# Zero matmuls ahead of TensorE's waits, forced ScalarE table switches, and a fully biased first batch in a fused attention and token-mixing kernel

## The chip, the cores and the metric

The kernel runs on one core of a Trainium2 chip. The metric is the device time of one execution, in microseconds (us). The kernel before took 180.71 us, the median of 8 runs that lie between 179.4 and 184.47 us. One execution was profiled. In the profile, PE is TensorE's matmul path, PEld its weight loads, DVE is VectorE, ACT ScalarE, POOL GpSimd and SP the queue engine. [...]

## The reference

Four batches of eight heads, 768 rows and a head width of 64 go through a sparse attention: a row sees the 8 global columns and the last 96 rows up to itself, with a bias that falls linearly with the distance. The attention's output, as a 768 by 512 matrix per batch, goes through a mixing block.

```
scores = scale * q @ k.T - slope[h] * dist        # masked to 8 global + 96 local columns
a = exp(scores) / sum(exp(scores));  x = a @ v     # per head, then heads side by side
theta = x @ w_theta                                # 512 x 512
y = w_tok_r @ (x * cos(theta)) + w_tok_i @ (x * sin(theta))   # 768 x 768 each
u = x + y
out = u + relu(u @ w_ch)                           # 512 x 512
```

## The kernel before, in words

**Tiling.** A batch `b` is cut into six tiles of 128 rows, and these into three groups `g` of two tiles. Heads are taken in four pairs `p`. Names of operations carry these numbers: `s012` is the score operation of batch 0, group 1, pair 2.

**A batch's operations.** `t` transposes q or k on PE (L377), and `q`, `k`, `kp` copy the result out of PSUM (L386); `kg` writes the global columns into it (L399). `s` computes scores (L452), `x` is the exponential on ACT (L475), `v` multiplies with the values on PE (L504), and `n` normalises on DVE (L515, L517). `vpa` and `vpb` build the previous tile's values (L413, L416). `xt` and `xc` transpose the result (L529, L532; by DMA in the last two batches). `th` is the matmul with w_theta (L547), `cos` and `sin` run on ACT (L556, L558), `z` multiplies on DVE (L568). `tw` and `twc` transpose the token weights once (L337, L342). `mx` is the token mixing (L589), `u` the sum (L601), `ut` and `uc` its transpose (L612, L616, or a DMA at L620), `ch` the channel matmul (L631), `o` the final step on DVE (L637) and `st` the store.

**The bias.** It comes into the scores in one of two ways. In a biased group (`BIASED`, groups 0 and 1 of batch 0) two matmuls `bi` per head pair put a multiple of a distance table `dtab` into PSUM first (L444), and the scores accumulate on it. Everywhere else, `m` multiplies the exponentials by a table `etab` = exp(-slope * dist) on DVE (L483). `etab` is made by eight activations at the start (L672).

**What sets the order.** The program is a flat list of operation names, `ORDER`, issued one by one; each name falls to one engine's queue, and a suffix such as `/ACT` chooses the engine of a copy. [...] The attributes `prio`, `lat`, `after` and `boost` belong to the planner that wrote the list and do nothing at run time. Loads go through POOL's queue in the order `load1` to `load81`; from `load20` a `gate` (L216) holds POOL until the load five places earlier has landed. Stores and DMA transposes go through SP's queue.

**Buffers.** PSUM has two rings of four banks, `pa` (scores and theta) and `pb` (all else). An operation that takes a bank waits for the reader of the bank's last user.

**The start.** `warm0` is eight matmuls of zeros (L326) while the first loads are under way. The first q and k tiles come as float32 over the SP and ACT queues (`hw`, L266) and are cast by `cast` (L273).

Of the kernel before, what the change touches and what calls it, by code (L numbers as in the profile page):

```python
# [15 lines left out]
class Plan:  # L16
# [3 lines left out]
    def __init__(self, pools):  # L20
        self.pools, self.ops = pools, {}
# [5 lines left out]
    def issue(self, order):  # L27
        assert sorted(n.split("/")[0] for n in order) == sorted(self.ops)
        for n in order:
            n, _, eng = n.partition("/")  # L30
            op = self.ops[n]
            op.took = eng or op.took
            op.fn()
# [3 lines left out]
hw00 hw10 ones1 zero rel ones2 halfpi ones3 warm0 ones4 ones6 ones0 ones5 load1 hw01 hw11 sid4 sid2 sid5 sid7  # L37
sid3 sid1 load2 sid0 sid6 far0 ident far1 load3 dtab0 cast00/DVE dtab1 load4 dtab2 cast10/DVE t0000 q000/DVE
load5 t0010 dtab3 k000/DVE kp000/ACT bi0000 bi0001 load6 bi0010 etab2 bi0011 kg000 cast01/DVE etab5 load7
t0001 cast11/DVE q001/ACT t0011 load8 etab7 kp001/DVE etab4 k001/DVE load9 kg001 etab6 s000 s001 load10 x0000  # L40
x0001 bi0020 load11 x0010 t0100 x0011 bi0021 s002 q010/DVE etab3 load12 t0110 x0020 bi0030 bi0031 k010/DVE
x0021 s003 load13 bi0100 etab1 kp010/DVE bi0101 load14 etab0 vpa00/DVE kg010 vpb00/DVE x0030 s010 load15 x0031
v002 v001 x0100 v000 load16 v003 vpa01/DVE x0101 bi0110 n000 bi0111 load17 s011 vpb01/DVE bi0120 load18 x0110
bi0121 n002 s012 x0111 load19 n003 bi0130 v010 x0120 bi0131 n001 s013 x0121 n010 t0200 x0130 t0210 x0131
q020/DVE v011 v013 k020/DVE kp020/ACT v012 n013 xt00 vpa02/DVE kg020 vpb02/DVE s020 xc00/DVE s021 x0200 n011
gate20 x0210 load20 n012 x0201 tw00 x0211 gate21 s022 m020 load21 twc00/ACT s023 m021 v020 x0220 xt01 n020
x0221 v021 gate22 th001 xc01/DVE load22 x0230 m022 x0231 th000 gate23 m023 load23 v022 cos000 tw10 n021 v023
gate24 twc10/DVE th010 load24 n023 gate25 tw11 n022 load25 th011 sin000 twc11/DVE cos001 gate26 z000 xt02
load26 sin001 tw01 xc02/DVE cos010 gate27 z001 twc01/ACT load27 th021 sin010 gate28 t1010 cos011 load28 z010
tw20 mx000 sin011 k100/DVE gate29 kp100/ACT load29 twc20/DVE tw21 th020 gate30 twc21/DVE load30 kg100  # L50
vpa10/DVE mx010 cos020 gate31 z011 load31 sin020 t1000 vpb10/DVE cos021 mx001 gate32 q100/DVE load32 sin021
z020 mx011 z021 gate33 s100 load33 s101 mx012 x1000 x1001 gate34 load34 x1010 mx002 m100 x1011 u01 gate35 s102
load35 s103 m101 x1020 u00 x1021 gate36 v100 x1030 load36 v101 n100 x1031 tw31 gate37 t1100 m102 twc31/ACT
load37 ut01 m103 t1110 q110/ACT uc01/DVE v102 gate38 k110/DVE v103 load38 ut00 kp110/DVE uc00/ACT tw40 tw30
gate39 kg110 twc40/DVE ch00 load39 twc30/ACT n102 tw41 gate40 n101 mx020 load40 twc41/DVE o00 s110 gate41
mx021 load41 vpa11/DVE x1100 st00 vpb11/DVE x1101 mx022 gate42 n103 load42 m110 xt10 u02 s111 gate43 xc10/ACT
load43 v110 t1200 n110 gate44 x1110 ut02 ch01 load44 q120/DVE x1111 uc02/DVE gate45 s112 m111 load45 s113
x1120 ch02 o01 gate46 x1130 load46 t1210 st01 x1121 o02 tw50 x1131 mx040 k120/DVE gate47 st02 kp120/ACT load47
m113 tw51 mx041 twc50/DVE gate48 twc51/ACT load48 kg120 m112 v113 s120 n113 gate49 v112 load49 x1200 mx050
n112 x1201 vpa12/DVE gate50 s121 m120 load50 s122 x1210 mx042 vpb12/DVE x1220 gate51 v120 x1221 load51 u04  # L60
mx052 x1211 m122 gate52 ut04 mx051 load52 uc04/DVE m121 v122 gate53 ch04 u05 load53 n120 v121 gate54 ut05 n122
v111 load54 uc05/ACT mx030 n121 n111 gate55 s123 load55 th101 vpa20/DVE x1230 vpb20/DVE x1231 gate56 o04 xt11
load56 th100 m123 xc11/ACT st04 gate57 v123 load57 cos100 mx032 n123 gate58 th110 load58 xt12 sin100 gate59
mx031 cos101 xc12/DVE load59 sin101 z100 ch05 gate60 cos110 u03 load60 th121 sin110 o05 gate61 th120 vpa21/DVE
load61 st05 vpb21/DVE t2010 z101 gate62 t2100 load62 k200/DVE kp200/ACT t2000 q210/DVE t2110 gate63 load63
th111 q200/DVE k210/ACT kp210/DVE t2200 gate64 cos111 load64 kg200 ut03 kg210 q220/DVE mx110 uc03/ACT gate65
z110 sin111 ch03 load65 cos120 z111 mx100 sin120 gate66 o03 load66 cos121 z120 t2210 st03 sin121 mx101 gate67
k220/DVE kp220/ACT load67 z121 s200 s201 gate68 mx111 vpa22/DVE x2000 load68 kg220 x2001 vpb22/DVE x2010 mx102
m200 gate69 x2011 load69 s202 m201 s203 mx112 u10 x2020 gate70 x2021 load70 x2030 ut10 v201 u11 v200 x2031
gate71 m202 s210 load71 ut11 n200 mx120 x2100 n201 gate72 x2101 mx121 load72 m203 m210 v203 gate73 s211 load73  # L70
vpa30/DVE v210 n203 x2110 mx122 gate74 x2111 n210 load74 s212 vpb30/DVE s213 u12 x2120 ch10 gate75 x2130 m211
load75 ut12 v202 x2121 ch11 o10 x2131 gate76 m212 load76 st10 s220 n202 v211 x2200 mx140 gate77 m213 x2201
load77 xt20 s221 n211 v212 gate78 m220 x2210 mx142 load78 x2211 n212 v220 m221 s222 gate79 load79 ch12 n220
x2220 x2221 vpa31/DVE gate80 s223 load80 vpb31/DVE v221 x2230 m222 mx130 x2231 gate81 n221 load81 v222 mx132
m223 n222 gate82 v223 load82 v213 n223 th201 n213 xt22 th200 o12 o11 mx131 cos200 xt21 mx150 u13 st12 mx152
sin200 ut13 vpa32/DVE cos201 mx151 z200 sin201 st11 mx141 u15 vpb32/ACT z201 th221 ut15 u14 th220 ut14 t3110
t3210 k310/DVE kp310/ACT th210 k320/DVE t3010 kp320/DVE cos210 t3000 k300/DVE sin210 t3100 q300/ACT kp300/DVE
th211 q310/DVE ch15 cos211 kg300 kg310 z210 sin211 ch14 o15 cos220 t3200 z211 sin220 st15 ch13 cos221 o14
sin221 z220 mx200 st14 q320/DVE s300 z221 s301 mx201 x3000 kg320 x3001 o13 x3010 mx202 m300 x3011 st13 s302
m301 s303 mx210 u20 x3020 x3021 x3030 ut20 v300 m302 mx212 x3031 n300 s310 m303 s311 x3100 mx211 x3110 v301  # L80
x3111 u21 mx220 x3101 n301 ut21 ch20 m311 s312 m310 s313 x3120 mx222 o20 x3121 st20 v303 x3130 mx221 m312
x3131 n303 v310 v311 u22 v312 ch21 n310 ut22 n312 mx240 o21 v302 mx242 n302 st21 n311 mx230 xt30 m313 s320
s321 x3200 mx231 x3210 v313 x3211 mx232 n313 x3201 m321 ch22 xt31 u23 s322 m320 s323 ut23 x3220 mx250 o22
x3230 v320 x3231 mx241 st22 n320 x3221 m323 mx252 u24 v323 m322 th300 ut24 n323 v322 cos300 v321 n322 th301
n321 mx251 xt32 sin300 ch23 u25 cos301 z300 ch24 sin301 ut25 o23 th310 z301 st23 th311 o24 cos310 sin310 st24
mx300 cos311 z310 th320 sin311 z311 th321 cos320 sin320 mx301 cos321 z320 mx310 sin321 z321 mx311 mx302 mx312
u30 ch25 ut30 u31 mx320 o25 ut31 mx322 st25 mx321 ch30 u32 mx330 ut32 o30 mx331 st30 mx332 ch31 u33 mx340 ut33
o31 ch32 st31 mx342 o32 mx341 st32 mx350 u34 mx352 ut34 mx351 ch33 u35 ut35 o33 ch34 uc35/ACT st33 ch35 o34
ch351 o35 st34 o351 st35 st351
# [4 lines left out]
def kernel(  # L94
# [44 lines left out]

    def act_t(n):  # L140
        return 0.06 + n * 0.00084
# [14 lines left out]
    BIASED = (0,1)  # L156
# [12 lines left out]
    zero = const.tile([T, 512], BF, name="zero")  # L169

    add("zero", {"DVE": 0.3}, lambda: nc.vector.memset(zero, 0.0), writes=["zero"], prio=-9)
    for i in range(NV):
        add(f"ones{i}", {"DVE": 0.07},
            lambda i=i: nc.vector.memset(v_bufs[i][:, :, :, D:D + 1], 1.0), writes=[("ones", i)], prio=-8)
    add("halfpi", {"DVE": 0.07}, lambda: nc.vector.memset(halfpi, math.pi / 2.0), writes=["halfpi"], prio=-8)
# [33 lines left out]
    def load(fn, us, ndesc, spot, depth=0, reads=(), writes=(), alloc=None):  # L209
# [4 lines left out]
        if depth:  # L214
            add(f"gate{n}", {"POOL": 0.35},
                lambda: nc.gpsimd.tensor_copy(out=scrap, in_=landed[n - depth]()),  # L216
                reads=[("ld", n - depth)], prio=-100 + n - 0.5, after=after)
            after = [f"gate{n}"]
        add(f"load{n}", {"POOL": 0.62 + 0.00028 * ndesc}, fn, reads=reads, writes=list(writes) + [("ld", n)],
            alloc=alloc, prio=-100 + n, lat=(1.05, us + {2: 0.75, 3: 0.75, 17: 1.1}.get(n, 0.0), 0.65), after=after)  # L220

    def load_qk(b, g, i, t, depth=0):
        key = ("qk", b, g)

        def fn():
            if key not in tiles:
# [501 lines left out]
```

## Time and profile before

| what | value |
|---|---|
| median of 8 runs | 180.71 us |
| the profiled execution's own time | 179.4 us |
| its span, first to last instruction | 177.6 us |
| PE busy | 161.3 us, 91% |
| DVE busy | 134.4 us, 76% |
| ACT busy | 107.0 us, 60% |
| POOL busy | 84.0 us, 47% |
| mean granted TensorE clock | 0.976 |

The profiled execution is the fastest of the eight. Its time is 1.8 us longer than its span. Matmuls overlap in the pipeline, so a busy PE is not a PE at its peak; how much work it does in a stretch is better counted in matmuls of a known pitch.

### The profile page before, as it was taken

The page shows a single profiled execution, that of the slowest core. Times are in us where ns is not written, and L with a number is a line of the kernel's source. Part 1 is how long each engine was busy: PE and PEld are TensorE (multiplying, and loading weights), DVE is VectorE, ACT ScalarE, POOL GpSimd, SP SyncE. Part 2 cuts the span into 40 slices and gives each one's busy share as a digit, 9 for nine tenths or more (in the row PEclk, how much of TensorE's full clock was granted, in tenths as well). Part 3 has the DMA queues.
Part 4 walks back from the last instruction along what each step waited for, and adds up shares of the span by engine and source line. Part 5 has one row for each costly group of instructions (what it writes and reads, how often), then busy time and mean ns, then how long its engine had stood idle before and what let it go on. Part 6 is the DMA issues. An engine that isn't in the chain of part 4 may idle for free.

```text
span 177.6 us, 4008 instructions
## 1 busy us (share of the span) xinstructions
PE 161.3 (91%) x1529; PEld 89.9 (51%) x1552; DVE 134.4 (76%) x315; ACT 107.0 (60%) x183; POOL 84.0 (47%) x150
## 2 busy tenths in 40 slices
PE   7469979898999999999697999999999999999991
PEld 2145656564856564474353554664554554444440
DVE  7726899887999988689599896798696787543442
ACT  2398869979937737858945667299741674600010
POOL 8998279849979999899799000000000000000000
PEclk9957999999999999999999999999999999999998
DMA  5999999999999999999999919404135656124514
GB/s 123 187 154 151 194 177 130 154 175 132 145 123 191 221 133 126 169 152 124 164 125 137 196 30 202 127 10 167 33 89 135 104 93 165 42 47 114 183 45 177
DMA packets 96868, 23.73 MB, mean 134 GB/s; under 512 B 91088, under 2 KB 93904, under 8 KB 96848
## 3 DMA queue, kind: packets, MB, share of 16 engines
q0 software_dynamic: 73504, 12.33, 97.0%
q1 hardware_dynamic: 21264, 10.62, 23.4%
q10 hardware_dynamic: 2080, 0.52, 1.6%
q8 instruction: 12, 0.20, 0.4%
q14 instruction: 8, 0.07, 0.1%
HBM read 25.69 MB, written 6.29 MB: 180 GB/s over the span
## 4 chain that ended last, share of the span: by engine, by line
PE 68%; DVE 11%; ACT 10%; DMA 5%; issue 3%; DVEq 0%; SPq 0%; ACTq 0%
PE pb L589 30%; PE pb L631 10%; PE pa L547 8%; PE pa L452 6%; ACT e L475 5%; PE pa L504 4%; PE pb L377 4%; DMA uT<-u 3%; DMA e<-in_q_dram 2%; DVE kk L386 2%; ACT kk L386 2%; DVE zri L568 1%; PE pb L337 1%; PE pa L444 1%; PE pb L529 1%
## 5 line engine op out<-in xcount | busy, mean ns | idle before, releaser
L589 PE MATMUL pb<-zri,w_tokT 128*128 128x512 bf16 x273 | 67.5, 379 | 1.1 <-issue 0.6
L475 ACT ACTIVATE e<-pa 128x512 bf16<-128x512 f32 (+1 forms) x96 | 46.7, 569 | 20.9 <-PE pa L452 20.8
L589 PEld LDWEIGHTS <-w_tokT 128*128 128x128 bf16 x288 | 25.8, 98 | 26.8
L483 DVE TENSOR_TENSOR e<-e,etab 128x1024 bf16<-128x1024 bf16 (+1 forms) x40 | 25.4, 644 | 4.3 <-ACT e L475 4.0
L601 DVE TENSOR_TENSOR u<-x,pb 128x512 bf16<-128x512 bf16 x24 | 16.4, 683 | 12.4 <-PE pb L589 12.4
L631 PE MATMUL pb<-w_ch_bf,uT 128*128 128x512 bf16 (+1 forms) x98 | 24.1, 371 | 1.2 <-DMA uT<-u 1.1
L547 PE MATMUL pa<-w_theta_bf,xT 128*128 128x512 bf16 x90 | 23.2, 379 | 0.8 <-DVE xT L532 0.5
L243 POOL DMA_DIRECT2D vn<-in_v_dram x24 | 21.5, 898 | 1.1 <-DMA qk<-in_q_dram 0.6
L556 ACT ACTIVATE cs<-pa,halfpi 128x512 bf16<-128x512 f32 x24 | 16.8, 700 | 6.6 <-PE pa L547 6.6
L452 PE MATMUL pa<-qT,kk 64*128 64x128 bf16 x352 | 17.9, 222 | 2.8 <-ACT e L475 1.7
L229 POOL DMA_DIRECT2D qk<-in_q_dram x22 | 19.6, 889 | 1.8 <-issue 1.2
L229 POOL DMA_DIRECT2D qk<-in_k_dram x22 | 19.3, 877 | 0.5 <-issue 0.4
L504 PEld LDWEIGHTS <-e 128*128 128x128 bf16 x352 | 14.7, 98 | 7.3 <-DVE e L483 1.4
L637 DVE SCALAR_TENSOR_TENSOR o<-pb,u 128x512 f32<-128x512 f32 (+1 forms) x25 | 16.3, 663 | 2.7 <-PE pb L631 2.7
L452 PEld LDWEIGHTS <-kk 64*128 64x128 bf16 x352 | 10.8, 95 | 14.9 <-issue 10.9
L568 DVE TENSOR_TENSOR zri<-x,cs 128x1024 bf16<-128x1024 bf16 x24 | 16.2, 683 | 2.7 <-ACT cs L558 2.7
L377 PE MATMUL pb<-ident,qk 128*128 128x128 bf16 x192 | 15.0, 231 | 2.7 <-DVE qk L273 2.7
L377 PEld LDWEIGHTS <-qk 128*128 128x128 bf16 x192 | 12.7, 103 | 7.8 <-DVE qk L273 4.2
L517 DVE TENSOR_TENSOR x<-pa,rec 128x256 bf16<-128x256 f32 x36 | 15.3, 424 | 1.2
L386 ACT COPY kk<-pb 128x1024 bf16<-128x1024 bf16 (+1 forms) x8 | 7.6, 960 | 13.0 <-DVE kk L386 13.0
L616 ACT COPY uT<-pb 128x512 bf16<-128x512 bf16 x4 | 2.4, 589 | 20.8 <-PE pb L612 20.8
L558 ACT ACTIVATE cs<-pa 128x512 bf16<-128x512 f32 x24 | 14.7, 611 | 0.0
(61 smaller groups left out, 193.4 us busy)
## 6 DMA issues: line engine op xcount, KB each, us to landing
out_dram<-o SPq DMA_DIRECT2D x23, 256.0 KB, 2.3
vn<-in_v_dram POOLq DMA_DIRECT2D x24, 128.0 KB, 4.9
qk<-in_q_dram POOLq DMA_DIRECT2D x22, 128.0 KB, 5.2
qk<-in_k_dram POOLq DMA_DIRECT2D x22, 128.0 KB, 5.0
w_nat<-in_moe_w_tok_r_dram POOLq DMA_DIRECT2D x6, 192.0 KB, 6.0
w_nat<-in_moe_w_tok_i_dram POOLq DMA_DIRECT2D x6, 192.0 KB, 6.4
e<-in_k_dram ACTq DMA_DIRECT2D x2, 256.0 KB, 5.9
e<-in_q_dram SPq DMA_DIRECT2D x2, 256.0 KB, 5.0
```

The lines of the kernel that those rows point to most:

```text
L229: nc.gpsimd.dma_start(out=tiles[key][:, i, t].rearrange("p (h d) -> p h d", d=D), in_=(q, k)[i][b, :, r0:r0 + T, :].rearrange("h p d -> p ...
L243: nc.gpsimd.dma_start(out=v_bufs[i][:, t, :, 0:D], in_=v[b, :, r0:r0 + T, :].rearrange("h p d -> p h d"))
L377: nc.tensor.transpose(p_[:, t - u0, p], tiles[key][:, i, t, p * T:(p + 1) * T], ident)
L452: nc.tensor.matmul(p_[hh][:, s], lhsT=tiles["kk", b, kg][R, kt, p, r, :], rhs=tiles["qT", b, g][R, qt, p, :], start=not biased, stop=not b ...
L475: nc.scalar.activation(tiles[ek][:, hh, 0:n], tiles[pb[hh]][:, 0:n], AF.Exp, scale=scale)
L483: nc.vector.tensor_mul(e_[:, :, 0:n], e_[:, :, 0:n], etab[:, 2 * p:2 * p + 2, s0:s0 + n])
L504: nc.tensor.matmul(o, lhsT=l_, rhs=r_, start=(i == 0), stop=(i == len(mms) - 1))
L547: nc.tensor.matmul(p_, lhsT=tiles["xT", b, g][:, p, t, :], rhs=w_theta_bf[:, p, :], start=(p == 0), stop=(p == NP - 1))
L556: nc.scalar.activation(tiles[ck][:, 0], tiles[ps], AF.Sin, bias=halfpi)
L568: nc.vector.tensor_mul(tiles[zk][:, t].rearrange("n i (p c) -> n i p c", p=NP), tiles["x", b, g][:, None, :, t, :].to_broadcast([T, 2, NP, ...
L589: nc.tensor.matmul(p_, lhsT=w_tokT[wi][:, 2 * g + t, tt * T:(tt + 1) * T], rhs=tiles["z", b, g][:, t, wi, :], start=(n == 1 and t == 0 and ...
L631: nc.tensor.matmul(p_, lhsT=tiles["uT", b, tt][:, p, :], rhs=w_ch_bf[:, p, i * w:(i + 1) * w], start=(p == 0), stop=(p == NP - 1))
```

## The change

Six edits come together.

- **Padding.** A suffix `+n` on a name in the order makes the operation put `n` zero matmuls ahead of its own, into the bank that it is about to use (`fill`). Where the operation is a transpose, the padding is 128-wide transposes of zeros; elsewhere it is a zero matmul as wide as the operation's output. Where the bank already holds a bias, zeros are added to it.
- **Forced table switches.** An activation of one element, `ts` (sine) or `tx` (exponential), stands at each change of ACT's function.
- **Batch 0 all biased.** Group 2 of batch 0 gets `bi` matmuls and loses its four `m`.
- **Engines of copies.** Among others `cast11`, `vpa02` and `vpb02` move from DVE to ACT, `kp000` and `q001` from ACT to DVE.
- **The start.** The distance table, and on ACT six of the eight `etab` activations, come ahead of the first copies; the first four `bi` come ahead of the first transposes.
- **A new order** everywhere else, with new latencies in the planner, which do nothing at run time.

```diff
+            n, _, pad = n.partition("+")
             n, _, eng = n.partition("/")
             op = self.ops[n]
-            op.took = eng or op.took
+            op.took, self.pad = eng or op.took, int(pad or 0)
             op.fn()
...
+    def fill(p_, acc=False):
+        for _ in range(plan.pad):
+            if p_.dtype == BF:
+                nc.tensor.transpose(p_, zero[:, 0:T], ident)
+            else:
+                nc.tensor.matmul(p_, lhsT=zero[:, 0:T], rhs=zero[:, 0:p_.shape[-1]], start=not acc, stop=not acc)
...
-    BIASED = (0,1)
+    BIASED = (0, 1, 2)
...
+        if b:
+            add(f"tx{b}", {"ACT": 1.36}, lambda: nc.scalar.activation(tiny, tiny, AF.Exp), reads=["tiny"],
...
+        add(f"ts{b}", {"ACT": 1.36}, lambda: nc.scalar.activation(tiny, tiny, AF.Sin), reads=["tiny"],
```

The first part of the new order, with all of its paddings:

```diff
+far1 load2 ident dtab0 sid5 sid6 sid1 load3 sid3 dtab1 dtab2 dtab3 sid4 load4 sid0 etab1 cast00/DVE bi0000
+etab2 bi0001 load5 bi0010 cast10/DVE bi0011 etab0 t0000 t0010 q000/DVE load6 etab4 k000/DVE kp000/DVE etab6
+load7 cast01/DVE etab7 kg000 t0001+27 load8 cast11/ACT q001/DVE etab3 load9 t0011+16 k001/DVE kp001/ACT load10
+etab5 kg001 s000+6 s001 load11 t0100 x0000 x0001 bi0020+1 q010/DVE load12 x0010 t0110 x0011 bi0021 bi0030
+k010/DVE kp010/ACT s002 load13 bi0031 s003 x0020 load14 vpa00/DVE x0030 bi0100+3 vpb00/DVE x0021 kg010 load15
+x0031 v001+2 bi0101 s010 load16 vpa01/DVE bi0110 x0100 bi0111 load17 s011 vpb01/DVE x0101 v003 v000 load18
+x0110 bi0120 n000 bi0121 x0111 s012 load19 n003 bi0130 x0120 bi0131 n001 s013 x0121 t0200 x0130 v012 q020/DVE
+v010 x0131 v011 n010 t0210+4 n012 vpa02/ACT k020/DVE v002+3 bi0200 n011 bi0201 bi0210 vpb02/ACT bi0211
+kp020/DVE v013 kg020 n002 s020+3 n013 s021 x0200 xt00 gate20 x0201 xt01 load20 xc00/DVE bi0220 x0210 v020
...
+twc10/DVE tw20+2 twc11/ACT th020 twc20/DVE gate28 sin010 z001 load28 tw21 cos011 th021 z010 gate29 sin011
...
+mx012 twc30/ACT gate34 load34 s100 u01 s101 mx002 x1000 gate35 x1001 load35 x1010 m100 s102+1 x1011 gate36 u00
+x1020 load36 s103+2 x1021 m101 v100+1 x1030 tw31 gate37 n100 load37 x1031 v101 ut00 twc31/DVE t1110 uc00/ACT
```

And the second change of batch, with `tx2`, beside the same stretch before:

```diff
-k220/DVE kp220/ACT load67 z121 s200 s201 gate68 mx111 vpa22/DVE x2000 load68 kg220 x2001 vpb22/DVE x2010 mx102
...
+gate65 kg210 o05 load65 sin121 z120 s200 tx2 st05 s201 gate66 mx111 z121 load66 mx112 x2000 gate67 x2001
```

## The prediction

> **What bounds the kernel now.** I read the engines' busy shares and the slices first, then the chain that ended last, then TensorE (PE) in narrow windows.
>
> ```profile
> PE 161.3 (91%) x1529; PEld 89.9 (51%) x1552; DVE 134.4 (76%) x315; ACT 107.0 (60%) x183; POOL 84.0 (47%) x150
> PEclk9957999999999999999999999999999999999998
> PE 68%; DVE 11%; ACT 10%; DMA 5%; issue 3%; DVEq 0%; SPq 0%; ACTq 0%
> ```
>
> PE is the bound, except where it waits or is slow: the clock digits fall to 5 and 7 in slices 3 and 4. Narrow windows (start:end, length, PE busy, ..., granted clock, DMA share, GB/s) place it:
>
> ```profile
> 8.50:9.00 0.50, 0.01 (x1) 0.01 (x1) 0.50 (x2) 0.50 (x2) 0.19 (x1) 0.81 2.42 154
> 9.50:10.00 0.50, 0.50 (x7) 0.30 (x6) 0.00 (x0) 0.36 (x1) 0.50 (x1) 0.50 2.44 155
> 15.60:16.00 0.40, 0.40 (x5) 0.07 (x4) 0.38 (x1) 0.40 (x1) 0.27 (x1) 0.96 3.23 151
> ```
>
> A mean of 0.81 in the first means that the clock halved at 8.81; 0.96 in the last, that it came back at 15.63. PE runs at half speed for 6.82 us. The chain there, in order of time:
>
> ```profile
> 7.40 0.59 ACT kk L386
> ...
> 8.99 0.62 PE pb L377 x4
> 9.63 0.59 ACT qT L386
> 10.22 1.89 ACT etab L672 x3
> 12.11 0.39 ACT e L475
> 12.54 0.48 PE pa L444
> 13.01 0.85 PE pb L377 x8
> 13.87 0.32 PE pa L444
> 14.19 0.44 PE pa L452 x6
> 14.62 0.98 PE pb L377 x8
> ```
>
> So the start is a chain through ACT, with three `etab` ahead of the first exponential (12.01), and through a slow PE.
>
> **PE as a sum.** Pitches at full clock, from the chain: four 512-wide matmuls 0.86 (0.216 each), eight transposes 0.45 (0.056), a score operation 0.33, a value operation 0.35; zero-padded rows use the same pitches, 384 wide 0.162. Adding these along the old order gives 29.6 us up to `s100` (first scores of batch 1, warm-up included) and 129.6 us after it. In the trace `s100` starts at 41.14 and PE ends at 173.1: 10 us are lost before `s100`, only 173.1 − 41.14 − 129.6 = 2.4 us behind it.
>
> **The change, part by part.**
>
> *Padding.* Before `s100`: 27+16+4+2 transposes x 0.056 = 2.7; 6+1 of 384 x 0.162 = 1.1; 3+2+3+3 of 512 x 0.216 = 2.4; together 6.2 us. Behind it (`s102`, `s103`, `v100`) 0.7. Free only where PE would wait.
>
> *Batch 0 biased.* Eight 512-wide bias matmuls add 1.7 us to PE; four multiplications leave DVE (683 ns each, 2.7 us), and the value matmuls then follow the exponential directly.
>
> *Order.* `mx012` and `tw30` (0.9 + 0.3) now precede `s100`. New PE sums: 29.6 + 6.2 + 1.7 + 1.2 = 38.8 to `s100`, and 129.6 − 1.2 + 0.7 = 129.1 behind it. With the same later loss the two kernels tie if `s100` comes at 41.6.
>
> *When `s100` comes.* The zero memset is now DVE's sixth, so the warm-up starts near 1.45: never idle, PE would be there at 40.25. I followed each wait with durations of the trace, at full clock. The same DVE work precedes `cast00` but for three small table copies; `dtab` is ready and `cast00` starts near 5.0 (4.93 before), the bias matmuls run under it. k's cast follows at 5.6 and the transposes end by 6.3. The 27 zero transposes run 6.3 to 7.8 while DVE casts q's second tile: hidden. `cast11` stands behind six `etab` of 0.66 on ACT, which begin at 4.9 instead of 7.9, and ends at 9.4; the 16 fit before it, and PE waits 0.4. `k001` ends at 10.0, six more zeros reach 10.6, and the first exponential starts near 11.2 (12.01 before) with only exponentials and one copy behind it. `kp010` holds ACT to 14.1, so `bi0100` waits 1.1 for its bank. From there PE hardly waits, which means that the padding of `bi0100`, `v001` and `s020` is on its path. The waits sum to 0.2 + 0.4 + 0.1 + 1.1 + 0.3 = 2.1 us, and `s100` comes at 42.35, 0.7 later than the tie. Bounds: no wait at all gives 40.25 (−1.4); 1.5 us more waits, one more each for the moved cast, k copy and v copy, 43.9 (+2.3). What the etab and clock gain, PE's own list takes back.
>
> If the cover of the zeros is gone (the data earlier than I think), their 6.2 us are the loss, which is in the sum already: PE is counted in full.
>
> *Copies moved to ACT.* `vpa02` and `vpb02` at 1.0 each fall between `x0131` (21) and `x0200` (24.8), where ACT idles: free. Behind them is only `x0200`; if PE is earlier, up to 0.5 us.
>
> *Forced switches.* The trace says that a load waits for nothing:
>
> ```profile
> L556 ACT ACT_TABLE_LOAD x4 | 5.1, 1283 | 0.1
> L475 ACT ACT_TABLE_LOAD x3 | 3.8, 1283 | 0.1
> ```
>
> The number of loads stays eight. Seven one-element activations are new; from the exponential's rows (603 ns at 512, 501 at 384) one costs about 0.2 us, 1.4 us on ACT in all (0 to 3), mostly beside PE. What counts is where the switch stands. At the change to batch 2 it sat behind three k and q copies, and PE then waited:
>
> ```profile
> 86.67 0.21 PE L452 MATMUL pa<-qT,kk 64*128 64x128 bf16 x1 [0.83 <-ACT e L475]
> 87.05 0.60 PE L452 MATMUL pa<-qT,kk 64*128 64x128 bf16 x6 [0.17 <-ACT e L475]
> 87.81 0.32 PE L452 MATMUL pa<-qT,kk 64*128 64x128 bf16 x5 [0.17 <-ACT e L475]
> ```
>
> `tx2` now follows the last sine directly, ahead of those copies: about 1.0 of these 1.2 us. ACT, by the sum above, waits for `s100` instead of PE for ACT, which saves the 0.4 before `v100`. Later loss then 1.0 instead of 2.4 (0 to 4: the order of three batches is new).
>
> *Loads.* POOL's list is the same; gates hold only for buffers, 0 (±1). DMA transposes of `u` for batch 1 still fall among loads; the two waits of PE for them (0.19 and 0.88) can shrink or double.
>
> The last stores stand in the same form as before, and SP's list has the same 23 stores of 256 KB, so what follows PE's end keeps its 4.5 us.
>
> Sum: +0.7 − 1.4 = −0.7: span 176.9, execution 178.7. That stands to 179.4, the fastest of eight; their median is 1.3 above. [...] If PE stays busy, the new kernel should feel less of it: I add 0.5 and predict **179.2 us**.
>
> [...] Of the 27 and 16 zeros every one is a transpose. The row: the clock came back at 15.63 after a window (12.2 to 15.6) in which transposes were 16 x 0.107 = 1.7 us and all else about 1.3; and the warm-up's zero matmuls, 0.43 apart, were followed by transposes at full pitch (four in 0.40 at 5.42), so zeros count. By the row the clock holds. [...] I take the row, mixed as it is.
>
> **The rivals.**
>
> *The clock falls anyway (slower).* Price: zeros ahead of `s000` +1.7, then transposes and bias of the first group at half pitch (0.45 → 0.86 twice, four bias matmuls +0.6): +2.8 at `x0020`, and nothing later gives it back. 179.2 + 2.8 = 182.0. [...]
>
> *PE carries the padding.* If waits before `s100` are 3.6 rather than 2.1 and the later loss stays 2.4, PE ends at 1.45 + 38.8 + 3.6 + 129.1 + 2.4 = 175.35, 2.25 above before: 179.4 + 2.25 + 0.5 = 182.1. For it: 8.7 us more PE work on a bound PE. Against: DVE and ACT are lighter where they led.
>
> *DMA sets the middle.* A transpose of `u` took 5.4 us of the chain (91.34 to 96.78) because loads fill the queues until 99. If the new order needs it earlier, PE waits 2 us more: 181.2. Against: there is other mixing work to issue.
>
> *The switch and order gain more.* Later loss 0, waits 1.2: 179.2 − 1.9 = 177.3. It lies in the main case's range.
>
> **How the numbers follow.** About 0.5% (0.9 us) is what a measurement can tell. Main case with the larger gain: 0.58, range 176.5 to 180.3. Clock falls: 0.18. PE carries: 0.14. DMA: 0.10. Of the main case 0.48 is below 179.8 and 0.10 between; of the others 0.03 faster, 0.06 within, the rest slower. Faster 0.51, same 0.16, slower 0.33. Range 176.3 to 183.0.
>
> **What would show it.** Right: granted clock 1.0 from 7 to 20; first exponential near 11.2; `s100` at 42 to 43; no wait of scores for exponentials at the change to batch 2. Wrong: a second 0.5 stretch with zero transposes 0.107 apart; `s100` past 43.5; PE idle for `uT` above 2 us; or gains of several us behind `s100`, where I see only 2.4.

## The result and the profile after

The changed kernel took 178.67 us, the median of 19 runs (177.09 to 181.37); the kernel before took 180.38 us in 56 runs beside them (178.99 to 184.47). The ratio is 0.9904, with a 95% interval of 0.9879 to 0.9929: about 1% faster. The forecast was 179.2 us. Medians here and below are of all executions, while the ratios leave out those that took over 1.5% longer than the fastest of the same kernel, so that the two need not agree.

The profiled execution of the changed kernel took 179.44 us, 0.8 above its median, and that of the kernel before 179.4, 1.0 below its own. So the two profiles have the same span, 177.6 us, and the gain of 1.7 us can't be read off by subtracting one from the other. It is read from where the stages begin and from second profiles of both kernels (a0 and e11 below).

The page of the changed kernel: busy times, the granted clock by slices, and the chain that ended last by engine.

```profile
PE 166.5 (94%) x1607; PEld 93.2 (52%) x1631; DVE 133.9 (75%) x310; ACT 108.9 (61%) x192; POOL 81.9 (46%) x150
...
PEclk9999999999999999999999999999999999999998
...
PE 40%; DMA 36%; POOL 6%; DVE 6%; issue 6%; ACT 4%; DVEq 0%; POOLq 0%; SPq 0%
```

PE is busier by 5.2 us, and the dip of the clock in slices 3 and 4 is gone. DMA held 5% of the chain before and holds 36% here. The chain in order of time (start, length, what) says which transfers:

```profile
32.55 7.26 DMA w_ch_bf<-in_moe_w_ch_dram
...
52.02 6.37 DMA w_nat<-in_moe_w_tok_r_dram
58.95 4.48 DMA qk<-in_q_dram
...
86.59 5.62 DMA uT<-u
...
99.05 6.48 DMA uT<-u
```

This chain runs through POOL's loads and gates, then through two transposes of `u`, and only behind 105 us through PE alone. It is tempting to say that the change made the loads a bound. The second profiles speak against that: there the kernel before (e11, first line) has more DMA in its chain than the changed kernel (a0, second line).

```profile
PE 43%; DMA 26%; POOL 13%; issue 7%; ACT 4%; DVE 4%; SPq 0%; DVEq 0%; POOLq 0%
PE 76%; DVE 7%; DMA 7%; ACT 6%; issue 1%; DVEq 0%; SPq 0%
```

In both kernels the way through the loads and the way through PE seem nearly equally long, so that the shares of the chain swing from one execution to the next. What a load costs is better read from the waits. PE's own list of waits (who was waited for: total, times, longest) in the changed kernel from 40 us on:

```profile
PE pb L654 <- DMA uT<-u: 1.3, 2, 0.6
PE pa L522 <- DVE e L500: 0.9, 2, 0.6
PE pb L391 <- DMA qk<-in_k_dram: 0.3, 1, 0.3
PE pb L654 <- DVE qT L400: 0.3, 1, 0.3
```

The scores' wait for ACT at the change to batch 2, 1.2 us before, isn't there any more. Here is the stretch in which the zeros stand, PE's timeline (start, length, line, operation, count):

```profile
6.54 1.67 PE L145 MATMUL pb<-ident,zero 128*128 128x128 bf16 x27
8.08 0.40 PE L391 MATMUL pb<-ident,qk 128*128 128x128 bf16 x4
8.31 1.06 PE L145 MATMUL pb<-ident,zero 128*128 128x128 bf16 x16
9.48 0.40 PE L391 MATMUL pb<-ident,qk 128*128 128x128 bf16 x4
9.72 1.14 PE L147 MATMUL pa<-zero 128*128 128x384 bf16 x6
10.79 0.51 PE L469 MATMUL pa<-qT,kk 64*128 64x128 bf16 x12
11.23 0.62 PE L391 MATMUL pb<-ident,qk 128*128 128x128 bf16 x8
```

27 zero transposes in 1.67 us and eight real ones in 0.62 are the full pitch. In the same view of the kernel before, eight took 1.03:

```profile
14.55 1.03 PE L377 MATMUL pb<-ident,qk 128*128 128x128 bf16 x8
```

The first exponential starts at 11.50, the first scores of batch 1 (`s100`) at 42.58.

### The profile page after: what moved, and what is told of

Its sections match the earlier page's. It is cut to its first block, busy times and chain, and to the rows that moved or that the text cites. A ratio compares the mean times of both kernels' runs of the same rounds, so it can differ in the third digit from the quotient of the medians.

```text
span 177.6 us, 4162 instructions
## 1 busy us (share of the span) xinstructions
PE 166.5 (94%) x1607; PEld 93.2 (52%) x1631; DVE 133.9 (75%) x310; ACT 108.9 (61%) x192; POOL 81.9 (46%) x150
## 4 chain that ended last, share of the span: by engine, by line
PE 40%; DMA 36%; POOL 6%; DVE 6%; issue 6%; ACT 4%; DVEq 0%; POOLq 0%; SPq 0%
PE pb L610 20%; PE pb L654 8%; DMA qk<-in_q_dram 7%; DMA uT<-u 7%; PE pa L567 6%; DMA w_theta_bf<-in_moe_w_theta_dram 5%; DMA w_ch_bf<-in_moe_w_ch_dram 4%; DMA vn<-in_v_dram 4%; DMA w_nat<-in_moe_w_tok_r_dram 4%; DMA w_nat<-in_moe_w_tok_i_dram 3%; POOL qk L240 3%; DMA qk<-in_k_dram 3%; PE pa L522 2%; PE pa L469 2%; POOL scrap L227 2%
## 5 line engine op out<-in xcount | busy, mean ns | idle before, releaser
L576 ACT ACTIVATE cs<-pa,halfpi 128x512 bf16<-128x512 f32 x24 | 16.5, 688 | 11.3 <-PE pa L567 9.4
L500 DVE TENSOR_TENSOR e<-e,etab 128x1024 bf16<-128x1024 bf16 (+1 forms) x36 | 22.5, 637 | 1.1 <-ACT e L492 1.1
L522 PEld LDWEIGHTS <-e 128*128 128x128 bf16 x352 | 15.2, 98 | 8.1 <-DVE e L500 1.5
L469 PEld LDWEIGHTS <-kk 64*128 64x128 bf16 x352 | 10.0, 94 | 12.4 <-issue 10.1
L469 PE MATMUL pa<-qT,kk 64*128 64x128 bf16 x352 | 16.0, 218 | 0.1
L391 PE MATMUL pb<-ident,qk 128*128 128x128 bf16 x192 | 14.4, 219 | 0.4 <-DMA qk<-in_k_dram 0.3
L654 PEld LDWEIGHTS <-uT 128*128 128x128 bf16 x100 | 8.9, 98 | 10.6 <-DMA uT<-u 1.3
L638 ACT COPY uT<-pb 128x512 bf16<-128x512 bf16 x5 | 2.9, 588 | 18.6 <-PE pb L634 18.6
L400 DVE COPY kk<-pb 128x1024 bf16<-128x1024 bf16 (+1 forms) x19 | 11.9, 641 | 2.4 <-PE pb L391 2.4
```

The lines of the kernel that those rows point to most:

```text
L469: nc.tensor.matmul(p_[hh][:, s], lhsT=tiles["kk", b, kg][R, kt, p, r, :], rhs=tiles["qT", b, g][R, qt, p, :], start=not biased, stop=not b ...
L500: nc.vector.tensor_mul(e_[:, :, 0:n], e_[:, :, 0:n], etab[:, 2 * p:2 * p + 2, s0:s0 + n])
L522: nc.tensor.matmul(o, lhsT=l_, rhs=r_, start=(i == 0), stop=(i == len(mms) - 1))
L576: nc.scalar.activation(tiles[ck][:, 0], tiles[ps], AF.Sin, bias=halfpi)
L654: nc.tensor.matmul(p_, lhsT=tiles["uT", b, tt][:, p, :], rhs=w_ch_bf[:, p, i * w:(i + 1) * w], start=(p == 0), stop=(p == NP - 1))
```

## The experiments

Times are medians. "exp 1" and "exp 2" are the starts of the first exponentials of batches 1 and 2, and "PE end" is the end of PE's last group, all three from the profiles. The experiments ran in three blocks, each on one chip with the kernel before beside it: a0 and e1 to e3 (the kernel before took 180.69 us in 38 runs), e4 to e7 (181.28 in 35), and e8 to e11 (180.16 in 11). The changed kernel itself ran beside the first block only, as a0.

| kernel | us | ratio to before, 95% interval | exp 1 | exp 2 | PE end |
|---|---|---|---|---|---|
| before, first profile | 180.38 | 1 | 41.82 | 86.12 | 173.87 |
| changed, first profile | 178.67 | 0.9904 (0.9879–0.9929) | 42.95 | 84.50 | 173.72 |
| a0_after | 178.50 | 0.9914 (0.9877–0.9951) | 43.54 | 83.61 | 173.05 |
| e1_nopad | 178.92 | 0.9904 (0.9872–0.9936) | 45.63 | 85.45 | 176.25 |
| e2_first3 | 178.09 | 0.9888 (0.9843–0.9933) | 42.08 | 83.01 | 172.61 |
| e3_oldpad | 179.56 | 0.9956 (0.9926–0.9987) | 40.21 | 86.59 | 174.15 |
| e4_newhead_oldrest | 181.33 | 1.0048 (1.0007–1.0089) | 42.99 | 88.10 | 175.56 |
| e5_oldhead_newrest | 181.35 | 0.9983 (0.9936–1.0030) | 46.45 | 86.70 | 176.07 |
| e6_no_forced | 178.94 | 0.9910 (0.9875–0.9944) | 43.93 | 84.03 | 172.74 |
| e7_depth7 | 178.38 | 0.9894 (0.9853–0.9934) | 42.95 | 83.26 | 172.69 |
| e8_nopad_late | 178.94 | 0.9895 (0.9847–0.9944) | 41.76 | 82.31 | 176.32 |
| e9_mult02 | 177.79 | 0.9870 (0.9831–0.9908) | 43.32 | 83.50 | 172.37 |
| e10_best | 176.10 | 0.9772 (0.9743–0.9800) | 40.85 | 81.25 | 170.19 |
| e11_before | 180.05 (one run) | – | 41.65 | 86.50 | 174.51 |

The profiled executions of e1 and e8 were among the longest of their kernels; their spans (180.1 us both) are not compared, only where they lost time. That of e5 (span 179.9) lies near its kernel's median.

### All padding off (e1_nopad), most of it off (e2_first3), padding alone (e3_oldpad), nothing changed (a0_after)

```
e1:  every "+n" taken out of the changed order
e2:  only t0001+27, t0011+16 and s000+6 stay
e3:  the old order, with  t0010+10  t0001+24  s000+3  s001+6
a0:  the changed kernel again
```

> The changed kernel without any padding; all else, the order too, as changed. [...] Rival (the padding is dead weight on a PE that is the bound; the new order brings the gain): 6.9 us of zeros go, so 1 to 3 us faster than the changed one (175.7 to 177.7).

> The changed kernel with only the first three paddings (27, 16 and 6, before the first scores). My theory: these alone hold the clock, because behind them PE has work enough; the later paddings (3.5 us of zeros) stand partly on PE's path (bi0100, v001, s020: 1.7 us), so 0.5 to 1.5 us faster than the changed kernel (177.2 to 178.2), and the granted clock stays 1.0 from 7 to 20 us. Rival (every padding is needed or free): the same within 0.4 us, or the clock falls in the gap that PE has near 14 to 15 us and it is slower by 1.

> The kernel before, its order kept, with zeros added in its own gaps only (10 before t0010, 24 before t0001, 3 before s000, 6 before s001; 3.4 us of PE work). My theory: the clock stays at 1.0 from 7 to 16 us, the transposes and scores there run at full pitch (eight transposes 0.45 instead of 0.85 to 0.98), and the time falls by 1 to 1.8 us, to about 178.9, nearly the changed kernel's. Rival (the clock at the start costs little since ACT is the chain there): within 0.5 us of before, 179.9 to 180.9.

> The changed kernel again, on this chip and in these rounds, as the measure for the others, and a second profile of it. My theory: 178.7 within 0.5, the clock at 1.0 from 7 to 20 us, first scores of batch 1 at 42.3 to 42.9. Rival (the first profile, which is as long as the one before, is typical and the gain is a matter of chance): 179.5 or more.

With the zeros the clock holds: in the profiles of the changed kernel, a0 and e2, transposes run at full pitch from about 7 us on (27 zeros in 1.67 us in the changed kernel), and the mean granted clock is 0.991 to 1.000 in all runs of the changed kernel. Without them (e1) it fell in the profiled execution, and the means of the 20 runs are 0.976 to 0.990. The windows of e1 (start:end, length, then PE, PEld, DVE, ACT and POOL busy, the granted clock, DMA share, GB/s):

```profile
9.00:11.00 2.00, 1.22 (x21) 0.84 (x22) 0.43 (x2) 1.69 (x4) 1.76 (x2) 1.00 2.48 154
11.00:13.00 2.00, 1.32 (x15) 1.02 (x13) 0.86 (x2) 2.00 (x5) 1.98 (x3) 0.70 2.47 154
13.00:15.00 2.00, 2.00 (x19) 0.85 (x16) 1.57 (x3) 0.99 (x2) 2.00 (x3) 0.50 2.43 155
```

A mean of 0.70 from 11 to 13, full before the fall and half behind it, puts the fall at 11.8. And yet e1 is as fast as the changed kernel: its PE has 6.9 us less work, and meets something else. Its timeline just ahead of `s100`, with the idle time before the operation and its releaser in brackets:

```profile
42.63 0.82 PE L348 MATMUL pb<-ident,w_nat 128*128 128x128 bf16 x6 [2.38 <-DMA w_nat<-in_moe_w_tok_r_dram]
```

That is `tw30`, which the new order puts ahead of `s100`. It needs token weights which POOL's queue has not brought yet; PE stood idle for 2.38 us, and the clock fell once more at the end of this wait (mean 0.63 from 42 to 44 us). So exp 1 is 2.7 us *later* than with 6.2 us of padding.

e2 stays at full pitch with the first three paddings alone. It saves 2.9 us of PE work up to `s100`, but exp 1 comes only 0.9 us earlier. Of the 2.0 us between, 1.5 are two waits that the changed kernel doesn't have, one for a copy on DVE and one for the load of `tw30`; a third wait, for a load of k, follows behind exp 1:

```profile
23.49 0.51 PE L467 MATMUL pa<-qT,kk 64*128 64x128 bf16 x12 [0.83 <-DVE kk L411]
33.66 0.51 PE L348 MATMUL pb<-ident,w_nat 128*128 128x128 bf16 x6 [0.71 <-DMA w_nat<-in_moe_w_tok_r_dram]
46.36 0.40 PE L389 MATMUL pb<-ident,qk 128*128 128x128 bf16 x4 [0.89 <-DMA qk<-in_k_dram]
```

Padding alone in the old order (e3) gains 0.4%, between its theory and its rival. Exp 1 comes 1.4 to 1.6 us earlier than in the two profiles of the kernel before, but exp 2 0.1 to 0.5 later. PE's list of waits behind 40 us shows what took the gain; the kernel before has no such line there:

```profile
PE pb L344 <- DMA w_nat<-in_moe_w_tok_r_dram: 1.4, 2, 0.8
```

The head can be made faster, and the gain is mostly given back to the loads behind it. In a0 exp 1 came 0.6 us later than in the first profile: its clock rose later, as the four bias matmuls ahead of the first transposes show (1.46 us at 5.26, against 0.83 at 5.27).

### New head with old rest (e4), old head with new rest (e5)

```
e4:  changed order up to s100, then the old order without ts1..ts3, tx2, tx3
e5:  old order up to s100, then the changed order
```

> The new order up to the first scores of batch 1 (s100; paddings, forced switches ts0 and tx1 and the biased batch 0 with it), then all remaining operations in the old order, without forced switches. My theory from the prediction's sum (s100 comes 1.4 later than before, 0.7 later than the tie, and the rest gains 1.4): this half alone gains nothing but the clock's steadiness, 0 to 1.3 us below before (179.4 to 180.7). Rival (the start is the gain, as the clock's rate and the freed ACT suggest): most of the gain, 178.4 to 179.2.

> The old order up to s100 (no padding there, batch 0 biased in two groups only, no ts0 and tx1), then the remaining operations in the new order with ts1, tx2, ts2, tx3, ts3 and the three paddings behind s100. My theory: about 1.0 to 1.4 us below before (179.3 to 179.7), from the switch to batch 2 and later waits. Rival (the gain is all in the start): within 0.5 us of before, 180.2 to 181.2.

The new head alone is a loss (0.5%), which neither theory nor rival had, and the old wait at the change to batch 2 is back. From e4's timeline:

```profile
88.64 0.21 PE L467 MATMUL pa<-qT,kk 64*128 64x128 bf16 x1 [0.83 <-ACT e L490]
89.03 0.60 PE L467 MATMUL pa<-qT,kk 64*128 64x128 bf16 x6 [0.17 <-ACT e L490]
89.79 0.32 PE L467 MATMUL pa<-qT,kk 64*128 64x128 bf16 x5 [0.17 <-ACT e L490]
```

Against the changed kernel, which shares its head (exp 1 at 42.99 and 42.95), e4's PE ends 1.84 us later (175.56 − 173.72), and the two ratios differ by 1.4%: that is what the new rest is worth behind the new head. Behind the old head it is not: e5 gains nothing that can be measured, and its timeline has e1's wait again. How many of its other executions have this wait is not known.

```profile
43.46 0.82 PE L348 MATMUL pb<-ident,w_nat 128*128 128x128 bf16 x6 [2.46 <-DMA w_nat<-in_moe_w_tok_r_dram]
```

The old head does less PE work ahead of `tw30`, comes to it earlier, and waits. The gain of the change is therefore no sum of parts: in this pair the rest gains only behind the head that comes late enough for the load of `tw30`.

### No forced switches (e6_no_forced)

```
-x0231 v022 th010 ts0 n022 ...   -load31 tx1 mx010 ...   (all seven ts, tx)
+x0231 v022 th010 n022 ...       +load31 mx010 ...
```

> The changed kernel without the seven one-element activations; each table load then stands directly before the first activation that needs it, which moves it behind the copies between. My theory: the load waits for nothing, so only its place counts; at the change to batch 1 and 2 the loads stand behind one to three copies, 0 to 1 us slower than the changed kernel (178.5 to 179.5). Rival (the forced switches do nothing but cost 0.2 us each): the same or up to 0.5 us faster.

Without `tx1` the load of the exponential's table slid from 39.14 to 42.64, and exp 1 from 42.95 to 43.93; the time did not change (0.9910). At the other changes the table loads moved by 0.01 to 0.99 us; at those to batches 2 and 3 the new order leaves ACT no copy between the last sine and the first exponential. The wait at batch 2 is gone in e6 too, so that the new places of sines and copies removed it, and not the tiny activation. In the kernel before one copy stands there, `kp220`, in front of the table load:

```profile
83.80 1.01 ACT L386 COPY kk<-pb 128x1024 bf16<-128x1024 bf16 x1 [0.87 <-DVE kk L386]
84.83 1.28 ACT L475 ACT_TABLE_LOAD   x1
```

### Loads issued earlier (e7_depth7)

```
-    DEPTH = 5
+    DEPTH = 7
```

> The changed kernel with the gates seven loads back instead of five, so POOL issues loads earlier; nothing else changes. New theory after the first runs (without padding PE waited 2.4 us for a load of token weights, so loads are the second bound and cover the padding): if the gate's distance sets when loads land, 0.5 to 2 us faster (176.5 to 178). Rival (the DMA engines are full, so earlier issue only lengthens the way): within 0.4 us of the changed kernel, with more us to landing.

The last load is issued at 88.8 us instead of 102.1, but the time is the same within the interval, as the rival had it. The earlier loads do free the later transposes of `u`. Those issued between 95 and 108 us take this long to land in the changed kernel and in e7:

```profile
DMA to landing us min/median/max: 6.5/6.6/6.6
DMA to landing us min/median/max: 2.4/2.4/2.4
```

Only the gates differ, so the loads are what makes these transposes long. But PE waits as long as before, now for a transpose that still falls among loads (1.41 us at 92.01; in the changed kernel two waits of 1.3 together).

### Is it the load that eats the gain? (e8_nopad_late)

```
-load33 tw30 q100/DVE mx012 twc30/ACT gate34 load34 s100 ...
+load33 q100/DVE mx012 gate34 load34 s100 ...
-m101 v100+1 x1030 tw31 gate37
+m101 v100 x1030 tw30 twc30/ACT tw31 gate37      (and every "+n" taken out)
```

> The changed kernel without any zero padding, and with the token-mixing products of block 3 (tw30, its copy twc30) moved from ahead of the first scores of batch 1 to behind their four groups. Without the move, PE waited 2.38 us there for the load of w_tok 3 and the first exponential of batch 1 came at 45.63. Theory (loads are the second bound, and the wait for this load ate what PE gained by doing no padding): the first exponential of batch 1 comes near 42 to 43, and the time falls by part of the 2.4 us, ratio to before near 0.984. Rival (the later parts of the kernel wait for loads too, so an early head only moves the wait): first exponential of batch 1 near 42 to 43, but other PE waits for q, k or token weights grow behind it and the ratio stays at 0.990. Second rival (the wait was a matter of that disturbed execution): first exponential near 43, ratio 0.990, and no waits grow.

The profile shows what the first rival expected, though the wait that grew is for a transpose and not for a load. With `tw30` out of the way exp 1 is at 41.76, 3.9 us earlier than in e1, and exp 2 3.1 us earlier. But PE ends where e1's does, and the ratio stays at 0.99. In this execution the time went into transposes of `u`:

```profile
106.90 1.89 PE L652 MATMUL pb<-w_ch_bf,uT 128*128 128x512 bf16 x4 [2.97 <-DMA uT<-u]
```

2.97 us idle in front of one group of channel matmuls, and the group itself took 1.89 us instead of 1.04: the clock had fallen again (mean 0.66 in the window 105 to 110). POOL still issues loads until 100.6, and the transposes issued between 95 and 108 take 7.9 to 8.8 us to land. The executions of e8, of which this was the longest, scatter from 177.25 to 181.94; that the shorter ones lose time in the same place is not shown.

### The third group with multiplications again (e9_mult02)

```
-    BIASED = (0, 1, 2)
+    BIASED = (0, 1)
-... x0201 ... bi0200 bi0201 ...
+... x0201 m020 ...               (bi02xx out; m02p right behind x02p1 for each pair p)
```

> The changed kernel with the third head group of batch 0 treated as before: eight 512-wide bias matmuls (bi02xx) left out of PE, four multiplications of 683 ns put back on VectorE ahead of its value products. The sum of the prediction: PE has 1.7 us less before the first scores of batch 1, VectorE 2.7 us more. If PE carries the head, the first exponential of batch 1 comes about 1.7 us earlier (near 41.3) and the ratio is near 0.985; if the value products then wait for VectorE instead (a little under 0.7 us each at the first), it comes near 42.5 and the ratio stays at 0.990; if loads are what the early head meets, it comes earlier but PE waits for a load ahead of it, and the ratio stays at 0.990.

exp 1 didn't come earlier (43.32), though PE has 1.7 us less to do: two value products now wait for the multiplications, as the second of the three expectations has it. The line from PE's list of waits in e9, which the changed kernel doesn't have:

```profile
PE pb L520 <- DVE e L498: 1.4, 2, 0.7
```

The ratio, 0.987, can't be told from the changed kernel's. What PE pays for the bias it gets back from DVE; no gain or loss by the edit can be told.

### The three together (e10_best) and the kernel before again (e11_before)

```
e10:  e2's order, with tw30 and twc30 behind s103 (as in e8) and DEPTH = 7
e11:  the kernel before, unchanged
```

> A candidate from what the runs showed: the changed kernel with only the padding ahead of t0001, t0011 and s000, seven load gates ahead instead of five, and the token-mixing products of block 3 behind the scores of batch 1. If the three small gains (0.3 to 0.4 us each, none clear alone) add up, the ratio to before is near 0.982 to 0.985; if they are the same wait taken away three times, it stays at 0.988 to 0.990.

> The kernel before once more, for a second profile. The first profile of it was 179.4 us, 1.3 below the median of its runs. If what the usual run loses lies in loads, this profile, if nearer the median, has longer waits of PE for w_tok, q, k or the transposes of u than the first one; if it lies in the clock, its half-speed stretch is longer than 6.82 us; if neither, the time around the span differs.

e10 beats both kernels: 176.10 us, 2.3% below the kernel before, and its six runs lie within 1.3 us (175.4 to 176.65), all of them below the fastest of the changed kernel (177.09). It is more than the 0.982 to 0.985 that a sum of the small gains would give. Less padding alone (e2), earlier loads alone (e7), and no padding with `tw30` moved (e8) were each 0.1 to 0.2% from the changed kernel, which is within the intervals; together the edits gain 1.3% on it (0.9772 / 0.9904; the two ratios are from different chips). This is what two bounds in turn would look like: less padding lets PE come earlier, which pays only if no load is in its way. Both load waits of e2, 0.71 and 0.89 us, are gone, and exp 1 is 1.2 us earlier than there. PE's waits in e10 from 40 us on:

```profile
PE pb L652 <- DMA uT<-u: 0.9, 1, 0.9
PE pb L652 <- DVE qT L398: 0.5, 1, 0.5
PE pb L608 <- issue: 0.3, 2, 0.2
PE pa L520 <- DVE e L498: 0.3, 1, 0.3
PE pa L467 <- ACT e L490: 0.2, 1, 0.2
```

No wait for a load is left. Whether two of the three edits would do isn't separated, and `tw30` moved with all padding in place wasn't run.

The second profile of the kernel before gave a surprise. The granted clock reads 1.00 in all windows of its head, and its PE is at half speed all the same. Windows of that profile, then its timeline:

```profile
5.00:10.00 5.00, 3.70 (x22) 2.09 (x23) 3.43 (x11) 2.41 (x5) 4.50 (x6) 1.00 2.05 173
10.00:15.00 5.00, 3.61 (x35) 2.44 (x33) 1.40 (x4) 4.59 (x11) 4.95 (x7) 1.00 2.45 154
```

```profile
6.62 1.48 PE L444 MATMUL pa<-dtab,sid 128*128 128x384 bf16 x4
...
10.68 0.61 PE L452 MATMUL pa<-qT,kk 64*128 64x128 bf16 x8 [0.31 <-DVE kk L386]
12.34 0.48 PE L444 MATMUL pa<-dtab,sid 128*128 128x384 bf16 x1 [1.06 <-ACT e L475]
12.61 1.06 PE L377 MATMUL pb<-ident,qk 128*128 128x128 bf16 x8
```

The four bias matmuls that take 1.48 us here took 0.81 in the first profile, and eight transposes in 1.06 is half pitch. PE was slow from its first matmul until about 16.5. In the first profile it was slow in the warm-up (eight matmuls in 3.60 us, 0.43 apart, here too), came up by 5.42, and was slow again from 8.81 to 15.63. The record shows only the second of these stretches: over the warm-up it reads 1.00 in eight profiles (both kernels' first ones, e1, e3, e5, e8, e10 and e11). So a half speed that stands from the beginning is what it misses here; why is not shown.

This longer slow stretch did not make the head later: exp 1 came at 41.65, against 41.82. What made the execution 0.7 us longer than the first lies between 41.65 and 122.72 (the first exponential of batch 3, 122.08 in the first profile). Its waits for transposes of `u` are 1.5 us on the DMA and 0.6 on ACT, against 1.1 and none. So what the usual run of the old kernel loses to its fastest one lay, in this one pair, where loads and transposes of `u` meet; more pairs were not profiled.

## Why the prediction was right

The side and the time were right (179.2 forecast, 178.67 measured), and most steps of the sum held in the first profiles; two terms were mis-sized, and the gain itself was larger than the sum made it.

- **The head's loss.** "`s100` comes at 42.35, 0.7 later than the tie": measured 42.58, so that the waits were 2.3 us rather than 2.1. The first exponential was at 11.50, forecast near 11.2. `bi0100` waited 1.08 us for its bank, forecast 1.1. The closeness is in part chance: in a0, where the clock rose later, the first exponential is at 12.09 and `s100` at 43.16, 2.9 us behind a PE that is never idle. e4 measures the head alone: a loss of 0.5%, or 0.9 us, with an interval that holds the 0.7.
- **The rest's gain.** "Later loss 1.0 instead of 2.4", with 0.5 us less PE work: 1.9 us. From `s100` to PE's end the old profile has 173.87 − 41.14 = 132.73 us, the new one 173.72 − 42.58 = 131.14: 1.6 us less. Between the second profiles it is 3.7 (133.54 in e11, 129.89 in a0), and against e4 1.84. So the gain is there, and its size is known to a microsecond or two only. (These ends of PE are those of its last group in the timeline; the forecast's 173.1 is 0.8 earlier, which drops out of the differences.) The wait named for it at the change to batch 2 went, as forecast. Not three copies stood ahead of the switch, though, but the one of 1.01 us shown above, and e6 shows that the order of sines and copies did the work and the tiny activations are worth nothing measurable. Their cost of 0.20 us each was right, as this line of the changed kernel's ACT shows:

```profile
31.86 0.20 ACT L691 ACTIVATE tiny<-tiny 1x1 f32<-1x1 f32 x1
```

- **The clock.** The prediction took the row, by which the clock holds, and it held. From 5.9 to 9.7 us PE did transposes and nothing else, 43 of zeros and 16 real ones. From 6.5 on all have the full pitch (27 zeros in 1.67 us, four real ones in 0.40), and so have the six zero matmuls behind them (1.14 us). What keeps the clock up behind 9.7 us is less clear: without the zeros (e1) it fell at 11.8, but every kernel with zeros ahead of the first scores has both the transposes and the six matmuls (nine in e3).
- **What the clock is worth: mis-sized.** "The new kernel should feel less of it: I add 0.5" puts a term into the sum that no run shows. What the two profiles of the kernel before show in its place: PE is slow in different stretches (from the start to about 16.5 us in one, from 8.81 to 15.63 behind the warm-up in the other), but exp 1 was the same to 0.2 us, and the 0.7 us came later. With the half speed behind the warm-up nearly gone (full pitch from 6.34 on, four transposes in 0.39 us), e3 gained 1.4 to 1.6 us up to exp 1 and 0.4% in all, as waits for loads took the rest. In the changed kernel the padding is worth nothing on balance (e1: 0.9904 with and without). The number came out well because two errors cancel. The sum stood on an execution 1.0 us below the old kernel's median, and its gain, 0.7, was 1.0 less than that between the medians, 1.7; the two alone give 178.7, and the 0.5 stands on top of them.
- **Loads: mis-sized.** "POOL's list is the same; gates hold only for buffers, 0 (±1)" holds for the changed kernel, whose PE waits 0.3 us for a load behind the start in one profile and not at all in the other, but not for its neighbours. An order that reaches `tw30` or a transpose of `u` earlier waits for them: 2.4 to 2.5 us in e1 and e5, 4.8 in e8 (two transposes). The 1 us of bounds was too small for such an order; what a load costs depends on how early PE comes. The old order put `tw30` behind batch 1's first scores; moving it ahead was costed at 0.3 us of PE work, which is its whole cost only because the padded head comes late enough.
- **Padding on PE's path.** It was counted in full as a loss, 6.2 us. As work that was right, as time it was not: part of it fills what would be waits, 0.8 us for a copy and 0.7 for a load in e2. Taking out the 2.9 us of it behind the first three stretches brings exp 1 only 0.9 us earlier there, but 2.1 in e10, where `tw30` is out of the way as well.
- **The biased third group.** +1.7 us on PE and −2.7 on DVE were right as work, and worth nothing that can be told as time (e9): without the bias, value products wait 1.4 us for the multiplications that stand in its place.

The rival "DMA sets the middle" named a mechanism that is there with the wrong outcome. PE waits 1.3 us for transposes of `u` in both profiles of the changed kernel, hardly more than before (1.1 and 1.5), and the loads decide only in versions that are earlier than this one.

## What to carry to other kernels

Where several edits gain nothing one by one, ask whether they push against two bounds in turn: here less padding, and loads issued earlier, moved the time by 0.1 to 0.2% each, and together with a load's consumer moved back by 1.3%, where which of the three is needed stayed open. Ahead of moving work earlier in a fixed order, look up when its operand lands, and what the longest wait behind it would be: a transfer that is hidden in the old order may be hidden by the work that the edit removes. Before the chain of one profile is called a change, look at a second profile of both kernels. What a half clock at the start costs is better measured by the start of the next stage than by the length of the slow stretch: in the kernel before, PE was slow to 16.5 us from its first matmul in one profile, and behind the warm-up from 8.81 to 15.63 in the other, and exp 1 came at 41.65 and 41.82.

## What was not expected of the hardware

- The granted clock in the records reads 1.00 in e11 while PE runs at half pitch (eight transposes in 1.06 us, four 384-wide matmuls in 1.48). It reads 1.00 over the warm-up too in the eight profiles named above, while its eight zero matmuls take 3.41 to 3.60 us. In these cases the pitch of a known group is the surer sign, and the mean clock of a run (0.971 to 0.999 in the eleven runs beside e11) is no full measure of how long PE was slow.
- Behind a single wait of PE in the middle of the kernel the half clock came back in three profiles: behind 2.38 us in e1 (mean clock 0.63 from 42 to 44 us), 2.46 in e5 (0.50 from 44 to 46), and 2.97 in e8 (0.66 from 105 to 110). Four 512-wide matmuls then took 1.91, 1.91 and 1.89 us instead of 1.04, so that these waits cost more than their own length. It did not come back behind e1's second one, 2.25 us at 95.03, where such a group took 1.04. In the changed kernel, whose longest wait behind the start is 1.1 us, no such drop is seen.
- DMA transposes of `u` issued between 95 and 108 us took 2.4 us to land in e7, whose last load is issued at 88.8, and longer where loads are issued later: 4.8 us in the first profile of the kernel before (last load at 97.0), 6.5 to 6.6 in the changed kernel (102.1), and 7.9 to 8.8 in e8 (100.6).
